# One-core Fourier mixing plus feed-forward kernel: pair 0 takes both slots through step B before mixing, and step B's loads change queue

## The chip, the cores and the metric

The kernel runs on one core of one Trainium2 chip. The metric is device time in microseconds of one execution, lower being better: the median of three runs, 1337.13 us before the change (1335.86 to 1338.55). The profile comes from one more execution of the same program.

## The reference, cut to what matters

```python
def _attn_ref(x, w_r, w_i, b_r, b_i):           # x: (4, 3008, 256)
    X = np.fft.rfft(x, axis=1)
    Yr = Xr @ w_r - Xi @ w_i + b_r
    Yi = Xr @ w_i + Xi @ w_r + b_i
    Yr, Yi = sign(Y) * max(abs(Y) - 0.01, 0)      # each of the two
    return np.fft.irfft(Yr + 1j * Yi, n=3008, axis=1)

def _moe_ref(x, w_in, w_out, alpha):             # x: (12032, 256)
    h = x @ w_in                                  # 2048 wide
    g = max(h, 0) + alpha * min(h, 0)
    return g @ w_out
```

A Fourier transform along the sequence, a complex 256 by 256 mix of the channels, a shrink by 0.01 towards zero, the transform back, and a two-layer feed-forward block. `w_in` and `w_out` arrive as 64-bit floats, and the kernel turns them into two 32-bit parts on the chip.

## The kernel before, in words

The sequence of 3008 is 47 x 64, so the transform is made in two steps. Step A (`a_load`, `a_mm`, `a_evac`, lines 339 to 406) multiplies groups of x rows by the 47-point table; for batch 0 its result stays on chip in `a0_s`, for the other batches it goes to DRAM (`ad`). Step B (`b_load`, `b_mm`, `b_evac`, `b_evac2`, lines 410 to 506) brings rows of it, 128 partitions at a time, into a tile `bt` (three buffers) and multiplies by a 64-point table `rb_s`. The 24 frequencies ("slots") are taken two at a time, as 12 pairs q. `m_mm` (line 508) mixes the channels of a pair, `m_evac` (line 542) shrinks, `c_mm` (line 588) takes the pair back through the 64-point table `cf_s`, and `c_evac` (line 606) copies it out and stores it to DRAM (`zd`). Step D then reads `zd` back for the feed-forward block, which fills the rest of the time.

The order of work is written out by hand, engine by engine, and every engine and every DMA queue runs what it was given in that order. Around the change it is this:

- Step A of batch 0 runs over 16 groups (loop at line 997). In the middle of it, `b_half(0, 0)` and `b_half(1, 0)` load the first halves of the row tiles of pairs 0 and 1 by GpSimd (POOL); after it, the second halves go by SyncE (SP), followed on SP by x rows of batch 1, table rows 4 to 11 of `rb_s`, and one `conv_load`. `b_load(0, 2)` goes by POOL.
- `keep_warm(WARM)` gives TensorE (PE) 38 small matmuls, and then the loop at line 1031 runs t = 0 to 12. At t = 0, `first_pair` (line 439) does pair 0: slot 0 (four matmuls, then two ScalarE and two VectorE instructions that split the result into a high and a low part), ten small matmuls, the bias, the mix of slot 0, slot 1, then step B of pair 1, and last the mix of slot 1.
- At each later t: `b_mm` of pair t, the load of pair t + 3, `c_evac` of pair t - 4 with its store, `b_evac` of pair t, `m_evac` of pair t - 2, `m_mm` of pair t - 1, `b_evac2` of pair t, `c_mm` of pair t - 3, and `pump(PT[t])`. At t = 1 four matmuls of step A of batch 1 are put in.
- `pump(n)` (line 310) emits n of the instruction groups that convert the weights. One piece of weights (a 512 KB load by `conv_load` on SP, into one of three buffers) takes four groups, and two pieces overlap: group 1 is VectorE L288 of the older piece with ScalarE L270 of the newer, group 2 is VectorE L271 of the newer, group 3 is ScalarE L282 and L283, VectorE L284 and GpSimd L285 of the older, group 4 is L291 (VectorE or GpSimd) and GpSimd L292 of the older with VectorE L272 of the newer. The very first piece has only its three first groups. `PT` says how many groups each t gets: 0, 0, then 3 for t = 2 to 10, and 4 at t = 11.
- `load_cf` (line 210) brings table parts for `c_mm` at t = 0, 3, 6 and 8, by POOL. `load_rb` brings table parts for step B at t = 3 and 5, by SP.
- After the loop `TAIL` runs the last evacuations and `c_mm` of pairs 10 and 11, and ten groups of step A of batch 1 (`a_fill`). Then the feed-forward steps begin, and what is left of the conversion is pumped into their first 32 (`PAT`, line 965); at step 23 `combine_mix` (line 224) makes the weights of the mix for the later batches.

Of the kernel before, what the change touches and what calls it, by code (L numbers as in the profile page):

```python
# [96 lines left out]
def fft_mix_moe(ctx, tc, x, w_r, w_i, b_r, b_i, w_in, w_out, alpha, la, rb, lc, rd, lf, cf, sel, out):  # L97
    nc = tc.nc
# [27 lines left out]
    def f(t):  # L126
        return t.bitcast(F32)
# [16 lines left out]
    cf_s = f(cw_s)  # L144
# [63 lines left out]
        nc.sync.dma_start(out=rb_s[:, n0:n1], in_=rb[:, n0 + at:n1 + at])  # L208

    def load_cf(n0, n1):  # L210
        nc.gpsimd.dma_start(out=cf_s[:, n0:n1], in_=cf[:, n0:n1])

    def load_lc():
        lc_s = const.tile([128, 2, NSLOT, 128], F32R, tag="lc", name="lc_s")
# [32 lines left out]
    def conv_load():  # L247

        m, i = divmod(conv_m[0], 2)
        conv_m[0] += 1  # L250
        k = conv_m[0] % 3
        raw = cw_s[:, NSLOT + 8 * k:NSLOT + 8 * k + 8].rearrange("p (k n) f -> p k (n f)", k=2)
        raw = raw.rearrange("p k (n w) -> p k n w", w=2)
        src = w_out.bitcast(U32)[256 * m:256 * m + 256] if i else w_in.bitcast(U32)[:, 512 * m:512 * m + 512]
        nc.sync.dma_start(out=raw.rearrange("p k n w -> p k (n w)"), in_=src.rearrange("(k p) f -> p k f", p=128))
        conv_raw.append((raw, m, i))
# [151 lines left out]
    bt, xs, xe, yc, ys = {}, {}, {}, {}, {}  # L408

    def b_half(q, h):  # L410
        if h == 0:
            bt[0, q] = work.tile([128, 2, C], F32, tag="bt", name="bt", bufs=3)
        src = a0_s.rearrange("(w s q) (h g) r c -> q h w s (g r) c", w=4, s=2, h=2)[q, h]
        for k in range(2):
            (nc.sync if h else nc.gpsimd).dma_start(out=bt[0, q][64 * h:64 * h + 64, k], in_=src[:, k])

    def b_load(b, q):
        t = work.tile([128, 2, C], F32, tag="bt", name="bt", bufs=3)
        if b == 0:
            src = a0_s.rearrange("(w s q) g r c -> q w s (g r) c", w=4, s=2)[q]  # L420
        else:
            src = ad[b].rearrange("(w s q) r c -> q w s r c", w=4, s=2)[q]

        for k in range(2):
            (nc.gpsimd if b == 0 else nc.sync).dma_start(out=t[:, k], in_=src[:, k])
        bt[b, q] = t

    def b_slot(t, ps, q, s):
        for ct in range(CT):
            PE.matmul(ps[:, s, ct], t[:, s, 128 * ct:128 * ct + 128], rb_s[:, 2 * q + s], start=True, stop=True)  # L430

    def b_mm(b, q):
        t = bt.pop((b, q))
        ps = ps_f.tile([128, 2, CT, 128], F32, tag="f", name="ps_b")
        for s in range(2):
            b_slot(t, ps, q, s)
        pb[b, q] = ps

    def first_pair():

        t = bt.pop((0, 0))
        ps = ps_f.tile([128, 2, CT, 128], F32, tag="f", name="ps_b")
        pm[0, 0] = pm0 = ps_h.tile([128, 2, C], F32, tag="h", name="ps_m")
        hi, lo = (work.tile([128, 2 * CT * 192], F32R, tag=tag, name=tag).rearrange("p (s k n) -> p s k n", s=2, k=CT)
                  for tag in ("Xh", "Xl"))

        def slot(s):
            b_slot(t, ps, 0, s)
            up, down = (slice(64, 192), slice(0, 64))
            A.activation(out=hi[:, s, :, up], in_=ps[:, s], func=AF.Copy)  # L450
            A.activation(out=hi[:, s, :, down], in_=ps[:, s, :, 64:128], func=AF.Copy, scale=-1.0)
            V.tensor_tensor(out=lo[:, s, :, up], in0=ps[:, s], in1=f(hi)[:, s, :, up], op=ALU.subtract)
            V.scalar_tensor_tensor(out=lo[:, s, :, down], in0=ps[:, s, :, 64:128], scalar=-1.0,
                                   in1=f(hi)[:, s, :, down], op0=ALU.mult, op1=ALU.subtract)

        def mixed(s):
            n = 0
            for a, ws in ((hi, 2), (lo, 1)):
                for i, o in ((0, 64), (1, 0)):
                    for ct in range(CT):  # L460
                        for w in range(ws):
                            n += 1
                            PE.matmul(pm0[:, s], a[:, s, ct, o:o + 128], mix[i][:, w, ct],
                                      start=False, stop=(s == 1 and n == 6 * CT))

        slot(0)
        keep_warm(MID)
        PE.matmul(pm0, *bias[0], start=True, stop=False)
        mixed(0)
        slot(1)  # L470
        b_mm(0, 1)
        b_evac(0, 1)
        mixed(1)

    def b_evac(b, q):
        ps = raw = pb.pop((b, q))
        hi = work.tile([128, 2 * CT * 192], F32R, tag="Xh", name="Xh")
        lo = work.tile([128, 2 * CT * 192], F32R, tag="Xl", name="Xl")
        xs[b, q] = hi, lo, ps
        if b == 0:  # L480
            hi, lo = (t.rearrange("p (s k n) -> p s k n", s=2, k=CT)[:, :, :, 64:192] for t in (hi, lo))
        else:
            hi, lo = (t[:, 0:512].rearrange("p (k s n) -> p s k n", s=2, n=64) for t in (hi, lo))
            ps = ps.rearrange("p s k (w n) -> p s (k w) n", w=2)
        A.activation(out=hi, in_=ps, func=AF.Copy)
        sv = None
        if b:
            sm = work.tile([128, 256], F32, tag="ot", name="sm", bufs=1)
            sv = sm, sm.rearrange("p (k s n) -> p s k n", s=2, k=CT)
            A.activation(out=sv[1], in_=raw[:, :, :, 64:128], func=AF.Copy)  # L490
        xe[b, q] = hi, lo, ps, sv
# [114 lines left out]
    def c_evac(b, q):  # L606
        ps = pc.pop((b, q))
        st = work.tile([128, 2, C], F32, tag="zst", name="zst", bufs=3)
        aside = b == 0 and q == NPAIR - 2
        if aside:  # L610
            V.tensor_copy(out=st, in_=ps)
        else:
            A.activation(out=st, in_=ps, func=AF.Copy)
        zdone.append(q)
        dst = zd[b][8 * q:8 * q + 8].rearrange("(s q) r c -> (q r) s c", s=2)
        if b == 0:
            (nc.sync if aside else nc.scalar).dma_start(out=dst, in_=st)
        else:
            stores.append((dst, st))

# [345 lines left out]
    NG = R // 2  # L966
    EARLY = 4
    FILL = 14
    C0 = 1
    PT = [0, 0, 3, 3, 3, 3, 3, 3, 3, 3, 3, 4]  # L970
    TAIL = [['me', 1], ['ce', 3], ['cm', 2], ['cm', 1], ['ce', 2], ['ce', 1], ['d'], ['f', 4], ['e'], ['f', 6]]
    WARM = 38
    MID = 10
    A1_TAGS = ("zst", "zst", "Yt", "zst", "bt", "bt", "bt", "Xh", "Xl", "Xh", "Xl", "zst", "zst", "Yc")
    X1_TAGS = {4: ("Yl", "Yl"), 5: ("os", "Yt"), 6: ("gl",) * 2}
    idle = const.tile([128, 128], BF16, name="idle")
# [1 line left out]
    def keep_warm(n):  # L978
        ps = ps_f.tile([128, 512], F32, tag="f", name="ps_idle")
        for _ in range(n):  # L980
            PE.matmul(ps[:, 0:128], idle, idle, start=True, stop=True)

    with tc.manual_schedule():
# [13 lines left out]
        for n, (b, g) in enumerate(seq):  # L997
            a_mm(b, g)
            if n >= 1:
                a_evac(*seq[n - 1])  # L1000
            if n == NG // 2:
                b_half(0, 0)
                b_half(1, 0)
            if n == NG:
                b_half(0, 1)
                b_half(1, 1)
                b_load(0, 2)
                a_load(1, 1)
                load_rb(4, 12)
                for _ in range(C0):  # L1010
                    conv_load()
                bias_parts()
        a_evac(*seq[-1])
        split_mix()
# [3 lines left out]
        def run(fn, q, *args):  # L1018
            if 0 <= q < NPAIR:
                fn(0, q, *args)  # L1020
# [10 lines left out]
        for t in range(NPAIR + 1):  # L1031
            if t == 0:
                first_pair()
            elif t > 1:
                run(b_mm, t)
            run(b_load, t + 3)
            run(c_evac, t - 4)
            if t > 1:
                run(b_evac, t)
            run(m_evac, t - 2)  # L1040
            if t > 1:
                run(m_mm, t - 1, ps_h)
            for g in range(2, EARLY) if t == 1 else ():
                a_mm(1, g)
                a_evac(1, g)
            if t:
                run(b_evac2, t)
            run(c_mm, t - 3)
            if t < NPAIR:
                pump(PT[min(t, len(PT) - 1)])  # L1050
            if t in (3, 5):
                load_rb(3 * t + 3, 3 * t + 9)
            if t in (0, 3, 6, 8):
                load_cf((t + 1) // 3 * 6, (t + 1) // 3 * 6 + 6)
            if t == 3:
                put()
            if t == 6:
                load_tables()
            if 7 <= t < 12:
                a_load(1, t - 5)  # L1060
            if t == NPAIR - 1:
                load_rb(0, 4)
            if t == 10:
                half(1)
                conv_m[1] = FT
# [159 lines left out]
        for k in range(len(spairs) + SLAG):  # L1225
# [7 lines left out]
            if k >= SLAG:  # L1233
                n, t = spairs[k - SLAG]
# [43 lines left out]
```

## Time and profile before

| what | value |
|---|---|
| median of three runs | 1337.13 us |
| the three runs | 1338.55, 1335.86, 1337.13 us |
| the profiled execution's own time | 1335.1 us |
| its span, first to last instruction | 1333.3 us |
| mean granted TensorE clock | 1.00 of full |

The span is 1.8 us shorter than the profiled execution's time, and that execution is 2.0 us below the median. Times in the rows are microseconds from the start of the span. In a timeline the first number is the start, the second the duration (first start to last end for several instructions), then the engine, the line of the kernel, the operation, the tiles written and read, the shapes and the count; a bracket gives idle time of the engine just before and what ended it. PE is TensorE's matmuls, PEld its weight loads, DVE VectorE, ACT ScalarE, POOL GpSimd, SP SyncE.

### The profile page before, as it was taken

The numbers are of one execution on the slowest core, as the hardware profiler recorded it, in microseconds if no ns is written. First come the engines' busy times: TensorE is split into PE (matmuls) and PEld (weight loads), VectorE is DVE, ScalarE is ACT, GpSimd is POOL, SyncE is SP. The second block draws the span as 40 slices with busy tenths as digits, with TensorE's granted clock in tenths as the row PEclk, the third lists the DMA queues.
The fourth block names the chain that finished last, engine by engine and source line by source line (L and its number), as shares of the span: only waits on it lengthen the run. The fifth ranks groups of instructions, "written<-read, shape, count | busy, mean of one in ns | idle before, by whom it ended". The sixth has DMA issues, their size and how long they took to land.

```text
span 1333.3 us, 22169 instructions
## 1 busy us (share of the span) xinstructions
PE 1322.0 (99%) x7868; PEld 1155.6 (87%) x7868; DVE 1045.5 (78%) x1858; ACT 729.8 (55%) x1442; POOL 381.4 (29%) x364
## 2 busy tenths in 40 slices
PE   9999999999999999999999999999999999999998
PEld 5977888888888888888789888988898889888988
DVE  3767866777787877687777888888888888888885
ACT  3566654655456554444555555555555555555654
POOL 3754652212221222221222222222222222222222
PEclk9999999999999999999999999999999999999999
DMA  8974333332243312121101101110111011101000
GB/s 220 255 219 136 108 107 103 118 117 78 72 134 96 111 65 72 52 76 36 37 13 40 28 10 32 29 29 10 31 29 29 10 31 29 29 10 31 17 16 25
DMA packets 103759, 89.74 MB, mean 67 GB/s; under 512 B 62446, under 2 KB 85849, under 8 KB 103648
## 3 DMA queue, kind: packets, MB, share of 16 engines
q1 hardware_dynamic: 95744, 77.68, 20.4%
q0 software_dynamic: 4912, 7.76, 2.1%
q10 hardware_dynamic: 2992, 2.88, 0.7%
q8 instruction: 62, 1.02, 0.3%
q14 instruction: 49, 0.40, 0.1%
HBM read 50.76 MB, written 34.34 MB: 64 GB/s over the span
## 4 chain that ended last, share of the span: by engine, by line
PE 90%; DVE 5%; issue 2%; ACT 1%; DMA 1%; SPq 0%; ACTq 0%; DVEq 0%
PE ps_h L712 37%; PE ps_o L739 10%; PE ps_o L737 10%; PE ps_o L738 10%; PE ps_m L534 6%; PE ps_d L633 4%; PE ps_o L906 3%; PE ps_b L430 2%; PE ps_a L387 2%; DVE q L724 1%; DMA rb_s<-tab_rb 1%; PE ps_c L602 1%; PE ps_c L603 1%; DVE conv L272 1%; PE ps_c L604 1%
## 5 line engine op out<-in xcount | busy, mean ns | idle before, releaser
L712 PE MATMUL ps_h<-yh,w 128*128 128x512 f32 (+1 forms) x1472 | 492.4, 389 | 2.4 <-DVE sq L811 1.6
L712 PEld LDWEIGHTS ps_h<-yh,w 128*128 128x128 f32 x1472 | 275.1, 188 | 58.2 <-DVE q L724 3.2
L712 PE MATMUL ps_h<-yl,w 128*128 128x512 f32 (+1 forms) x736 | 284.9, 387 | 0.0
L840 POOL TENSOR_TENSOR l<-t,h 128x512 fp32r<-128x512 f32 x98 | 127.0, 1296 | 449.7 <-ACT h L838 430.2
L811 DVE SCALAR_TENSOR_TENSOR sq<-sq,beta_s,ps_h 128x512 f32<-128x512 f32 (+1 forms) x240 | 166.2, 724 | 59.1 <-ACT sq L810 58.8
L726 ACT ACTIVATE gh<-q 128x512 fp32r<-128x512 f32 x144 | 91.0, 632 | 160.7 <-DVE q L724 160.7
L729 POOL TENSOR_TENSOR gl<-q,gh 128x512 fp32r<-128x512 f32 x69 | 93.4, 1354 | 255.8 <-ACT gh L726 193.7
L712 PEld LDWEIGHTS ps_h<-yl,w 128*128 128x128 f32 x736 | 138.9, 189 | 21.7 <-DVE yl L684 0.2
L724 DVE SCALAR_TENSOR_TENSOR q<-q,beta_s,ps_h 128x512 f32<-128x512 f32 x144 | 107.0, 743 | 61.2 <-ACT q L723 59.8
L810 ACT ACTIVATE sq<-ps_h 128x512 f32<-128x512 f32 (+1 forms) x240 | 131.8, 577 | 31.0 <-PE ps_h L712 27.1
L826 ACT ACTIVATE dh<-sq 128x768 fp32r<-128x768 f32 x98 | 83.0, 847 | 108.5 <-DVE sq L811 81.3
L723 ACT ACTIVATE q<-ps_h 128x512 f32<-128x512 f32 x144 | 85.3, 592 | 79.9 <-PE ps_h L712 77.8
L838 ACT ACTIVATE h<-t 128x512 fp32r<-128x512 f32 x98 | 62.0, 633 | 105.2 <-DVE t L836 101.8
L737 PE MATMUL ps_o<-gh,w 128*128 128x512 f32 x288 | 114.5, 398 | 0.0
L739 PE MATMUL ps_o<-gl,w 128*128 128x512 f32 x288 | 112.7, 391 | 0.3 <-POOL gl L729 0.3
L738 PE MATMUL ps_o<-gh,w 128*128 128x512 f32 x288 | 112.8, 392 | 0.0
L835 DVE TENSOR_TENSOR dl<-sq,dh 128x768 fp32r<-128x768 f32 x98 | 93.2, 951 | 0.0
L729 DVE TENSOR_TENSOR gl<-q,gh 128x512 fp32r<-128x512 f32 x75 | 60.0, 800 | 42.3 <-ACT gh L726 41.5
L739 PE MATMUL ps_o<-l,sw_a 128*128 128x256 f32 x294 | 82.7, 281 | 0.0
L737 PE MATMUL ps_o<-h,sw_a 128*128 128x256 f32 x294 | 82.0, 279 | 0.0
L832 DVE TENSOR_TENSOR t<-sq 128x512 f32<-128x512 f32 x98 | 67.6, 690 | 2.9
L839 DVE TENSOR_TENSOR l<-t,h 128x512 fp32r<-128x512 f32 x98 | 67.0, 684 | 0.0
(199 smaller groups left out, 2969.7 us busy)
## 6 DMA issues: line engine op xcount, KB each, us to landing
zt<-zd SPq DMA_DIRECT2D x32, 384.0 KB
zd<-zst SPq DMA_DIRECT2D x37, 256.0 KB
ad<-ast SPq DMA_DIRECT2D x48, 192.0 KB
bt<-ad SPq DMA_DIRECT2D x72, 128.0 KB
out<-oT SPq DMA_DIRECT2D x248, 32.0 KB
xt<-in_x SPq DMA_DIRECT2D x21, 320.0 KB
cw_s<-in_moe_w_in SPq DMA_DIRECT2D x8, 512.0 KB
cw_s<-in_moe_w_out SPq DMA_DIRECT2D x8, 512.0 KB
```

The lines of the kernel that those rows point to most:

```text
L712: PE.matmul(ps, wi_h[m // FH][:, w, ct, 128 * (m % FH):128 * (m % FH) + 128], a[ct][:, 0:n], start=(k == 0), stop=(k == 3 * CT - 1))
L723: A.activation(out=q, in_=ps, func=AF.Relu, scale=-1.0)
L724: V.scalar_tensor_tensor(out=q, in0=q, scalar=beta_s[:, m:m + 1], in1=ps, op0=ALU.mult, op1=ALU.add)
L726: A.activation(out=hi, in_=q, func=AF.Copy)
L729: return lambda: (V if by_v else G).tensor_tensor(out=lo, in0=q, in1=f(hi), op=ALU.subtract)
L737: PE.matmul(o, wh, gh, start=first, stop=False)
L738: PE.matmul(o, wl, gh, start=False, stop=False)
L739: PE.matmul(o, wh, gl, start=False, stop=last)
L810: A.activation(out=q[:, j], in_=ps, func=AF.Relu, scale=-1.0)
L811: V.scalar_tensor_tensor(out=q[:, j], in0=q[:, j], scalar=beta_s[:, m:m + 1], in1=ps, op0=ALU.mult, op1=ALU.add)
L835: V.tensor_tensor(out=dl, in0=q[:, HS:], in1=f(dh), op=ALU.subtract)
L840: G.tensor_tensor(out=l24, in0=t24, in1=f(h24), op=ALU.subtract)
```

## The change

Seven edits.

1. `b_half`: pair 0's second half goes by POOL, and only pair 1's stays on SP.
2. `b_load`: from pair 3 on the rows of batch 0 go by SP instead of POOL. `load_cf`: the three later table parts go by SP instead of POOL.
3. `first_pair`: slot 0, six small matmuls instead of ten, slot 1, bias, mix of slot 0, mix of slot 1, and then step B of pair 1.
4. `c_evac`: the stores of pairs 6 and 7 (at t = 10 and 11) are issued by POOL instead of ACT.
5. The first `conv_load` moves from ahead of the loop to t = 0, behind the row load of pair 3.
6. `PT` gives t = 1 three groups instead of none, so that each later t has the groups that t + 1 had, and t = 11 has groups 4, 1, 2, 3 where it had 1, 2, 3, 4. The conversion after the loop has four groups less to do.
7. `C0` and its loop go.

```diff
     def load_cf(n0, n1):
-        nc.gpsimd.dma_start(out=cf_s[:, n0:n1], in_=cf[:, n0:n1])
+        (nc.sync if n0 else nc.gpsimd).dma_start(out=cf_s[:, n0:n1], in_=cf[:, n0:n1])
...
         for k in range(2):
-            (nc.sync if h else nc.gpsimd).dma_start(out=bt[0, q][64 * h:64 * h + 64, k], in_=src[:, k])
+            (nc.sync if h and q else nc.gpsimd).dma_start(out=bt[0, q][64 * h:64 * h + 64, k], in_=src[:, k])
...
         for k in range(2):
-            (nc.gpsimd if b == 0 else nc.sync).dma_start(out=t[:, k], in_=src[:, k])
+            (nc.gpsimd if b == 0 and q < 3 else nc.sync).dma_start(out=t[:, k], in_=src[:, k])
...
         slot(0)
         keep_warm(MID)
+        slot(1)
         PE.matmul(pm0, *bias[0], start=True, stop=False)
         mixed(0)
-        slot(1)
+        mixed(1)
         b_mm(0, 1)
         b_evac(0, 1)
-        mixed(1)
...
-            (nc.sync if aside else nc.scalar).dma_start(out=dst, in_=st)
+            (nc.sync if aside else nc.gpsimd if 6 <= q < 8 else nc.scalar).dma_start(out=dst, in_=st)
...
-    C0 = 1
-    PT = [0, 0, 3, 3, 3, 3, 3, 3, 3, 3, 3, 4]
+    PT = [0, 3, 3, 3, 3, 3, 3, 3, 3, 3, 3, 4]
...
-    MID = 10
+    MID = 6
...
                 load_rb(4, 12)
-                for _ in range(C0):
-                    conv_load()
                 bias_parts()
...
             run(b_load, t + 3)
+            if t == 0:
+                conv_load()
             run(c_evac, t - 4)
```

## Rows read from the trace of the kernel before

**Rows 1.** The page's first part: busy time of each engine.
```profile
PE 1322.0 (99%) x7868; PEld 1155.6 (87%) x7868; DVE 1045.5 (78%) x1858; ACT 729.8 (55%) x1442; POOL 381.4 (29%) x364
```

**Rows 2.** The timeline of PE from pair 0's first slot on.
```profile
23.27 0.67 PE L430 MATMUL ps_b<-rb_s,bt 128*128 128x128 f32 x4
23.78 0.72 PE L981 MATMUL ps_idle<-idle 128*128 128x128 bf16 x10
24.31 0.48 PE L468 MATMUL ps_m<-bias_p,ones 128*128 128x512 f32 x1
24.62 0.64 PE L463 MATMUL ps_m<-wr_s,Xh 128*128 128x256 f32 x4
...
28.80 0.72 PE L463 MATMUL ps_m<-wr_s,Xh 128*128 128x256 f32 x4
...
30.30 1.88 PE L387 MATMUL ps_a<-xt,lf_s 94*96 94x512 f32 x4
32.02 1.06 PE L430 MATMUL ps_b<-rb_s,bt 128*128 128x128 f32 x8
32.83 0.48 PE L514 MATMUL ps_m<-bias_p,ones 128*128 128x512 f32 x1
...
38.08 0.71 PE L430 MATMUL ps_b<-rb_s,bt 128*128 128x128 f32 x4 [0.84 <-DMA bt<-a]
...
41.70 1.03 PE L596 MATMUL ps_c<-Y,cw_s 128*128 128x256 f32 x4
42.56 1.05 PE L430 MATMUL ps_b<-rb_s,bt 128*128 128x128 f32 x8
...
47.39 1.05 PE L430 MATMUL ps_b<-rb_s,bt 128*128 128x128 f32 x8
...
61.89 1.05 PE L430 MATMUL ps_b<-rb_s,bt 128*128 128x128 f32 x8
...
67.23 1.05 PE L430 MATMUL ps_b<-rb_s,bt 128*128 128x128 f32 x8
```

**Rows 3.** Waits from 20 to 40 us: total us, times, longest.
```profile
PE ps_b L430 <- DMA bt<-a: 1.9, 4, 0.8
```

**Rows 4.** DMA issues by POOL near 1.3, 14 and 21 us: us to landing.
```profile
lf_s<-tab_lf POOLq DMA_DIRECT2D x1, 35.2 KB, 2.9
...
bt<-a POOLq DMA_DIRECT2D x4, 64.0 KB, 7.3
...
bt<-a POOLq DMA_DIRECT2D x2, 128.0 KB, 4.6
```

**Rows 5.** The timeline of POOL where pair 2's rows are issued.
```profile
20.87 1.34 POOL L425 DMA_DIRECT2D bt<-a  x2 [4.32 <-issue]
```

**Rows 6.** Waits from 60 to 66 us.
```profile
PEld ps_m L521 <- POOL Xh L500: 0.3, 1, 0.3
```

**Rows 7.** Timelines of DVE and of ACT, t = 8 and t = 11.
```profile
66.80 0.68 DVE L291 TENSOR_TENSOR conv<-conv,w 128x512 f32<-128x512 f32 x1
...
68.06 2.35 DVE L288 SCALAR_TENSOR_TENSOR conv<-cw_s,conv 128x512 uint32<-128x512 uint32 x1
...
81.64 0.81 DVE L288 SCALAR_TENSOR_TENSOR conv<-cw_s,conv 128x512 uint32<-128x512 uint32 x1
...
85.68 0.68 DVE L548 SCALAR_TENSOR_TENSOR Y<-ps_m,Yc 128x512 f32<-128x512 f32 x1
...
82.48 0.63 ACT L282 ACTIVATE w<-conv 128x512 fp32r<-128x512 f32 x1 [2.01 <-DVE conv L288]
...
84.61 0.69 ACT L547 ACTIVATE Yc<-ps_m,lam_s 128x512 f32<-128x512 f32 x1 [0.44 <-ACT zst L613]
```

**Rows 8.** Waits from 160 to 184 us.
```profile
PEld ps_h L712 <- DVE q L724: 2.0, 4, 0.6
```

**Rows 9.** Stretch of only SP row loads (batch 1): engines' us, clock, DMA, GB/s.
```profile
164.00:167.00 3.00, 3.00 (x14) 2.17 (x13) 2.97 (x6) 1.19 (x3) 0.97 (x2) 1.00 0.24 81
```

**Rows 10.** The same view over four pairs of the loop, t = 4 to 7.
```profile
42.00:61.00 19.00, 19.00 (x148) 18.43 (x147) 16.13 (x22) 12.32 (x21) 16.13 (x20) 1.00 0.92 234
```

## The prediction

> **What bounds the kernel now.** I read the page's first part, then the timeline of PE from pair 0 on, then the waits of that stretch. PE is busy 99% of the span [rows 1], so time can only come out of holes in PE's own sequence or out of work taken from it. From t = 4 on PE runs pair after pair without a hole: the first matmuls of pairs 4 and 5 stand 4.83 us apart, from 42.56 to 47.39 [rows 2], and that is what the matmuls need. Before that PE is late. The path from slot 0 to pair 4, piece by piece [rows 2]: a slot 0.51 (23.27 to 23.78), ten small matmuls 0.53, the bias 0.31, one mix 1.50 (28.80 to 30.30), step B of a pair 0.81 (32.02 to 32.83), four matmuls of step A 1.72 (30.30 to 32.02). One pair of the loop is 4.83, or 3.97 without its `c_mm` (0.86, from 41.70 to 42.56). In the old order that is 2 x 0.51 + 0.53 + 0.31 + 2 x 1.50 + 0.81 + 1.72 + 3.97 + 4.83 = 16.19, but the rows stand 19.29 apart. So 3.1 us are waits, and the largest cause named is rows of `bt` that have not landed [rows 3], last at 38.08 for pair 3 [rows 2]. Later holes, at t = 8, t = 12 and about 175 us, are read with the parts that touch them.
>
> **The change, part by part.** The terms are called A to E.
>
> **A, the start (edits 1, 2, 3, 5).** The new order is the old path with six small matmuls for ten, 0.32 for 0.53, and is 15.98 long. Slot 1 now runs while ScalarE and VectorE split slot 0, and pair 1's rows are asked for after both mixes, so those loads get 3 us more. Pair 3's rows are issued by SP behind slot 1, ahead of the weights instead of behind three loads of them. If nothing waits, 3.1 + 0.2 = 3.3 us go. What is late next is slot 0 itself: its second half now goes by POOL. POOL's next issue stood at 20.87 [rows 5]; the halves move to this place. From issue to landing POOL's loads took 2.9 us for 35 KB, 4.6 for 128 KB, and 7.3 for 64 KB while x was still being loaded [rows 4]. Between the first two by size, 64 KB land 3.4 later, at 24.3, against the old start of 23.27: 1.0 us lost. I take this because x is in by then. Slot 1's half is issued 0.67 later (half of 1.34 [rows 5]) and is asked for 0.83 later, so it is covered. A = -3.3 + 1.0 = -2.3; with 2.9 it is -2.8, with 4.6 it is -1.1, with 7.3 it is +1.6.
>
> [...]
>
> Pair 2's rows by POOL start 1.34 us later, at 22.2, and land near 26.8 by the 4.6 [rows 4, 5]; they are asked for at 24.3 + 0.51 + 0.32 + 0.51 + 0.31 + 3.00 + 0.81 + 1.72 = 31.5. Pair 3's are issued near 25.6 and asked for at 35.5. Both are covered.
>
> **B, POOL relieved (edit 2).** From pair 8 to pair 9 the cycle is longer: 61.89 to 67.23 is 5.34, 0.5 over 4.83 [rows 2], and the wait named is for POOL's negation of the high part [rows 6], which in the code stands behind a table load (t = 6) and a row load (t = 7) on POOL. Both leave POOL. B = -0.5; at least 0.
>
> **C, the last pairs (edits 4, 6).** At t = 11 the groups come as 4, 1, 2, 3. ScalarE's L282 waits for VectorE's L288, and behind it on ScalarE stand the copy of pair 8 and the shrink of pair 10, on which the last two `c_mm` wait with nothing else for PE to do. In the old order L288 came first, 81.64 to 82.45, L282 began at 82.48 and the shrink (L547) at 84.61, while VectorE came to its part (L548) at 85.68 [rows 7]. Where group 4 comes first, at t = 8, L288 ended 3.61 after L291 began (66.80 to 70.41), 2.80 later than with L288 first. L547 then ends at 84.61 + 2.80 + 0.69 = 88.1, 2.4 after 85.68. Against it: L288 itself was held to 2.35 there, 1.5 above the 0.81 of t = 11 [rows 7], with a GpSimd instruction beside it that ran late behind POOL's loads; and the store of pair 7 leaves ScalarE, about 0.4. POOL has no such loads now, so I take 1.0 of the 1.5 and all of the 0.4 off: 2.4 - 1.0 - 0.4 = +1.0. Ends: 0 and +2.4. POOL pays for two stores (0.67 each by [rows 5]) where it no longer has row loads: nothing.
>
> **D, four groups less after the loop (edit 6).** From 160 to 184 us the weight loads of L712 wait 2.0 us in four places for VectorE [rows 8]; that is where the last pieces of weights and `combine_mix` want VectorE, ScalarE and GpSimd together. With the conversion over some three steps sooner they no longer meet. Weight loads run ahead of the matmuls, so 2.0 is an upper end; D = -1.0, ends -2.0 and 0. The three groups at t = 1 cost PE nothing as long as their weights are there: ScalarE and VectorE have no more than one pair's split to do.
>
> **E, what SP now carries (edits 2, 5).** SP's queue gets nine pairs' rows (256 KB each) and three table parts, between the weights, x rows and stores of `ast` that it had. Each row load waits for a free `bt`, and the weights stand behind it; if they are late, ScalarE stands at L270 with the split of the next pair behind it. What a row load costs by SP shows in batch 1, where for 3 us nothing else moved: 0.24 of the 16 engines busy and 81 GB/s [rows 9], so as if four engines worked, and 256 KB take about 3.2 us. Over t = 4 to 7 the engines were 0.92 busy at 234 GB/s [rows 10], of which POOL's rows were 256 KB in 4.83 us, 54 GB/s. The rest is 0.92 x 180 / 234 = 0.71; if it is even over the engines, those four get 0.71 + 3.2 / 4.83 = 1.37 of a pair, 1.8 us too much in each of six pairs (t = 3 to 8), 10.7 in all. Against it, busy time includes waiting for one another, rows are asked for three pairs (14.5 us) after their issue, and weights about 1.3 pairs (6.4 us) after theirs. Of the two ends, 0 and 10.7 less the 3.4 that are left of those 6.4 after a landing of 3, 7.3, I take the lower with a little of the upper: E = +0.7.
>
> [...]
>
> **Sum.** -2.3 - 0.5 + 1.0 - 1.0 + 0.7 = -2.1. The profiled execution took 1335.1 us (1333.3 of span), so it would take 1333.0. It stands 2.0 below the median of 1337.1, and the forecast for the median is 1335.0. The runs of before lie 2.7 us apart, 0.2%, which is also about what a measurement of this kernel tells from no change.
>
> **Rivals.**
> - **Faster: C and E cost nothing.** Without POOL's loads VectorE is not held and reaches the last groups early, and the row loads hide in their three pairs of lead. For: PE has no hole from 42 to 61 us although the engines were 0.92 busy [rows 10]. Against: the order of the groups at t = 11 is fixed, and L282 is behind L288 in any case. The sum is -2.3 - 0.5 - 1.0 = -3.8: 1333.3.
> - **Slower: the row loads fill their four engines.** Place: t = 7 to 11. Price: E at 7.3 instead of 0.7, 1341.6. It decides once those engines have over 4.83 + 3.4 / 6 = 5.4 us of work per pair; by [rows 9, 10] it is 1.37 x 4.83 = 6.6 if all busy time is work, and (0.66 + 0.47) x 4.83 = 5.5 if a third of the 0.71 is waiting, so the point is near. Against: the lead of three pairs, and that PE had no hole while all 16 engines stood at 0.92.
> - **Slot 0 late.** The first halves, on the same queue, took 7.3 us [rows 4]. If the second do, A is +1.6 and the time 1338.9. Against: x had been loaded by 20 us.
>
> **How the numbers follow.** Forecast 0.45, the faster rival 0.38, the slower 0.10, slot 0 late 0.07. Faster by over 0.2% is 0.38; within it are the forecast and most of the last, 0.50; slower 0.12. The range takes A at -2.8, D at -2.0 and C and E at 0, 1331.8, and on the other side slot 0 late, 1338.9. Outside are the slower rival and as much again.
>
> **What would show it.** A: pair 4's first matmul near 40.3 instead of 42.56, slot 0 near 24.3, no wait for `bt` at pair 3. B: cycles of 4.83 throughout. C: the last `c_mm` about 1 us further behind pair 11's mix than before. D: no wait of L712 between 165 and 180. E: no ScalarE wait at L270 for weights. Wrong would be slot 0 after 25.5, cycles of over 5 us at t = 7 to 11, or a wait of PE for `bt` after pair 3.

## The result, and the profile after

| | before | after |
|---|---|---|
| median, us | 1336.86 (6 runs, 1335.17 to 1338.55) | 1350.57 (6 runs, 1347.46 to 1357.7) |
| ratio | | 1.0107, 95% interval 1.0081 to 1.0134 |
| span of the profiled execution, us | 1333.3 | 1345.7 |

The change costs 13.7 us, 1.1%. The forecast was 1335.0, and its range ended at 1338.9. The profiled execution of after is the quickest of its six (1347.46 us), so what follows explains 12.4 us of span.

The busy time of PE is 2.6 us above that of [rows 1]: the work is the same, and the time went into holes (stretches in which PE waits) and, for a small part, into matmuls at a lower clock (0.64 from 28 to 32 us, 0.50 from 56 to 60).

The first part of the page of after:
```profile
PE 1324.6 (98%) x7864; PEld 1159.8 (86%) x7864; DVE 1044.1 (78%) x1857; ACT 731.2 (54%) x1442; POOL 371.7 (28%) x348
```

To see where, set the same work of both kernels side by side. The timeline of PE of after, as in [rows 2]:
```profile
24.52 0.68 PE L430 MATMUL ps_b<-rb_s,bt 128*128 128x128 f32 x4 [0.87 <-issue]
...
26.78 0.68 PE L430 MATMUL ps_b<-rb_s,bt 128*128 128x128 f32 x4 [1.24 <-DMA bt<-a]
27.22 0.58 PE L469 MATMUL ps_m<-bias_p,ones 128*128 128x512 f32 x1
...
31.90 1.05 PE L430 MATMUL ps_b<-rb_s,bt 128*128 128x128 f32 x8
...
43.29 1.05 PE L430 MATMUL ps_b<-rb_s,bt 128*128 128x128 f32 x8
...
62.63 1.05 PE L430 MATMUL ps_b<-rb_s,bt 128*128 128x128 f32 x8
...
72.29 1.05 PE L430 MATMUL ps_b<-rb_s,bt 128*128 128x128 f32 x8
77.12 1.05 PE L430 MATMUL ps_b<-rb_s,bt 128*128 128x128 f32 x8
...
88.28 1.05 PE L430 MATMUL ps_b<-rb_s,bt 128*128 128x128 f32 x8
...
112.08 3.76 PE L633 MATMUL ps_d<-rd_s,zt 96*128 96x94 f32 x32
```
Three rows of the same view of the kernel before that did not stand in [rows 2] (pairs 6 and 11, and step D):
```profile
52.22 1.05 PE L430 MATMUL ps_b<-rb_s,bt 128*128 128x128 f32 x8
...
76.89 1.05 PE L430 MATMUL ps_b<-rb_s,bt 128*128 128x128 f32 x8
...
98.14 3.76 PE L633 MATMUL ps_d<-rd_s,zt 96*128 96x94 f32 x32
```

| first matmul of | before | after | later by | since the row above |
|---|---|---|---|---|
| slot 0 | 23.27 | 24.52 | 1.25 | |
| pair 4 | 42.56 | 43.29 | 0.73 | -0.52 |
| pair 6 | 52.22 | 62.63 | 10.41 | **+9.68** |
| pair 9 | 67.23 | 77.12 | 9.89 | -0.52 |
| pair 11 | 76.89 | 88.28 | 11.39 | +1.50 |
| step D | 98.14 | 112.08 | 13.94 | **+2.55** |
| end of span | 1333.3 | 1345.7 | 12.4 | -1.5 |

Nearly eight tenths of the net loss stand between pairs 4 and 6. The waits of after from 48 to 58 us name the chain:
```profile
ACT zst L613 <- DMA ad<-ast: 7.0, 1, 7.0
DVE Y L548 <- ACT Yc L547: 6.9, 1, 6.9
PEld ps_m L514 <- DVE Y L548: 6.2, 1, 6.2
PE ps_m L514 <- DVE Y L548: 6.0, 1, 6.0
```
Read it from the bottom: PE's mix waits for VectorE's shrink, that for ScalarE's, and ScalarE stands at L613, the copy of pair 0 out of PSUM. L613 needs one of the three `zst` buffers. Groups 0, 1 and 3 of step A of batch 1 sit in them (`A1_TAGS`) until their stores `ad<-ast` have landed. These stores are `put()` at t = 3, on SP. The timeline of SP of after shows what they stood behind:
```profile
39.55 1.15 SPq L425 DMA_DIRECT2D bt<-a  x2
42.98 0.37 SPq L255 DMA_DIRECT2D cw_s<-in_moe_w_out  x1
43.40 0.46 SPq L208 DMA_DIRECT2D rb_s<-tab_rb  x1
43.91 0.43 SPq L211 DMA_DIRECT2D cw_s<-tab_cf  x1
44.38 3.64 SPq L334 DMA_DIRECT2D ad<-ast  x4
```
Before, the same four stores were issued at 28.61 and L613 ran at 43.11 without a wait. Now they come 15.8 us later, behind row loads that wait for a free `bt` and behind a piece of weights whose buffer ACT L283 gave back only at 42.3 to 43.0 (ScalarE had stood 3.37 us before it for another piece). Once issued they were slow too: from the first issue to L613 (53.12) it is 8.74 us. Three stretches of 1 us inside the hole (busy time by engine, then granted clock, DMA share, GB/s):
```profile
51.00:52.00 1.00, 0.00 (x0) 0.00 (x0) 0.00 (x0) 0.00 (x0) 0.00 (x0) 1.00 0.28 110
52.00:53.00 1.00, 0.00 (x0) 0.00 (x0) 0.00 (x0) 0.00 (x0) 0.00 (x0) 1.00 0.26 101
53.00:54.00 1.00, 0.00 (x0) 0.00 (x0) 0.00 (x0) 0.60 (x1) 0.00 (x0) 1.00 0.26 97
```
Every compute engine waits, and the DMA engines are a quarter busy. That looks like SP's row loads in [rows 9] (0.24 at 81 GB/s), but from 51 to 53 us no row load moves. A row load puts 1 KB into each partition, and when row loads moved alone, from 41 to 43 us, all 181 packets were under 2 KB; these stores move 2 KB per partition, the table parts ahead of them 3 KB. From 51 to 53 us the only packets under 2 KB are 19 that are also under 512 B, too small for a row load's 1 KB. The packets of 51 to 53 us, and below them those of 41 to 43 us, when row loads moved alone:
```profile
DMA packets 107, 0.21 MB, mean 106 GB/s; under 512 B 19, under 2 KB 19, under 8 KB 107
...
DMA packets 181, 0.18 MB, mean 91 GB/s; under 512 B 4, under 2 KB 181, under 8 KB 181
```
What stood behind row loads in SP's queue was itself down to a quarter of the engines (0.26 to 0.28). Whether these are the engines that the row loads had kept busy stays open: the trace does not name engines.

After the hole the granted clock, 1.00 from 51 to 54 us, was at 0.50:
```profile
56.00:60.00 4.00, 3.80 (x17) 3.71 (x18) 3.86 (x6) 2.76 (x5) 3.10 (x3) 0.50 0.66 202
```

The other places: the waits of ACT of after from 24 to 104 us show ScalarE standing for weights seven times; between pairs 9 and 11 that is 1.50 us of PE's time.
```profile
ACT conv L270 <- DMA cw_s<-in_moe_w_in: 10.0, 4, 4.1
ACT zst L613 <- DMA ad<-ast: 7.0, 1, 7.0
...
ACT conv L270 <- DMA cw_s<-in_moe_w_out: 5.7, 3, 3.4
```
And from 160 to 184 us, where [rows 8] had 2.0 us:
```profile
PEld ps_h L712 <- DVE q L724: 0.2, 1, 0.2
```

### The profile page after: what moved, and what is told of

Same layout as the page of the kernel before. It is cut to its first block, busy times and chain, and to the rows that moved or that the text cites. A ratio compares the mean times of both kernels' runs of the same rounds, so it can differ in the third digit from the quotient of the medians.

```text
span 1345.7 us, 22143 instructions
## 1 busy us (share of the span) xinstructions
PE 1324.6 (98%) x7864; PEld 1159.8 (86%) x7864; DVE 1044.1 (78%) x1857; ACT 731.2 (54%) x1442; POOL 371.7 (28%) x348
## 4 chain that ended last, share of the span: by engine, by line
PE 93%; DVE 3%; DMA 2%; ACT 1%; issue 1%; SPq 0%; ACTq 0%; POOL 0%; DVEq 0%
PE ps_h L712 37%; PE ps_o L739 11%; PE ps_o L737 11%; PE ps_o L738 11%; PE ps_m L534 6%; PE ps_d L633 4%; PE ps_b L430 3%; PE ps_o L906 3%; PE ps_a L387 2%; PE ps_m L521 1%; DMA ad<-ast 1%; PE ps_c L602 1%; PE ps_c L603 1%; PE ps_c L604 1%; DVE q L724 1%
## 5 line engine op out<-in xcount | busy, mean ns | idle before, releaser
L712 PE MATMUL ps_h<-yh,w 128*128 128x512 f32 (+1 forms) x1472 | 492.2, 389 | 2.1 <-DVE sq L811 1.6
L712 PEld LDWEIGHTS ps_h<-yh,w 128*128 128x128 f32 x1472 | 275.1, 188 | 57.4 <-DVE q L724 2.3
L712 PE MATMUL ps_h<-yl,w 128*128 128x512 f32 (+1 forms) x736 | 284.9, 387 | 0.0
L712 PEld LDWEIGHTS ps_h<-yl,w 128*128 128x128 f32 x736 | 138.9, 189 | 21.7 <-DVE yl L684 0.2
```

The source lines that it names most:

```text
L712: PE.matmul(ps, wi_h[m // FH][:, w, ct, 128 * (m % FH):128 * (m % FH) + 128], a[ct][:, 0:n], start=(k == 0), stop=(k == 3 * CT - 1))
```

## The experiments

Each kernel was timed in five rounds beside the kernel before; medians are in us, and each ratio is to the kernel before.

**1. The stores earlier, by POOL.** The first theory: the stores' place on SP is the cause.
```
 after:  -            if t == 3:
         -                put()
         +            if t == 1:
         +                put(nc.gpsimd)
```


> The changed kernel with the four stores of step A (ad<-ast) issued at t = 1 by POOL instead of at t = 3 by SP. Theory 1, the stores stand on SP behind row loads and weights and hold the zst buffers: the hole of PE from 50 to 56 us goes whole, the wait of ACT L613 for ad<-ast goes, pair 6 starts near 53 us instead of 62.88, and the time falls by 7.6 to 9.7 us, to 1341 to 1343. Theory 2, SP's row loads fill their engines and make the weights late, and the stores are only the wait that happened to end last: ACT stands at L270 for weights instead, a hole of 3 us or more stays between pairs 4 and 6, and the time stays above 1346.

Measured: 1348.25, ratio 1.0102 (1.0071 to 1.0133). The hole went: pair 6 starts at 55.01. But by step B of pair 11 (87.47) the gain is down to 0.8 us of after's 88.28. (The profiled execution, 1356.16, is 8 us above the median; it lost them at a lower clock, 0.62 from 98 to 104 us and 0.50 from 104 to 116, see the last section.) The waits of ACT from 24 to 104 us:
```profile
ACT conv L270 <- DMA cw_s<-in_moe_w_in: 12.0, 4, 4.4
ACT conv L270 <- DMA cw_s<-in_moe_w_out: 11.4, 4, 4.5
```
15.7 us of waiting for weights became 23.4. Theory 1 was right about the hole and wrong about the time: two lines of supply were late, and the stores had hidden the weights.

**2. Edit 1 undone.**
```
 after:  -(nc.sync if h and q else nc.gpsimd)
         +(nc.sync if h else nc.gpsimd)
```


> The changed kernel with the second half of pair 0's rows by SP again (edit 1 undone). Theory 1, the start lost 1.25 us on slot 0, 1.24 on the wait for slot 1 and 1.3 on mixes at the lower clock, and the hole at 50 to 56 us follows from the chain that begins with step B of pair 1, so it moves with the start: slot 0 at 23.3, granted clock 1.00 from 27 to 32, pair 4 near 39.5, pair 6 near 59, time 1347 (3.8 lower). Rival, the hole's end is set by SP's transfers and not by PE: pair 4 near 39.5 but pair 6 still at 62 to 63, time within 1 us of 1350.6.

Measured: 1351.47, ratio 1.0113 (1.01 to 1.0126). Slot 0 came at 23.97, but slot 1 waited 3.40 for its rows instead of 1.24, the clock was 0.60 from 28 to 32, and pair 4 came at 44.92. The time is the rival's, but neither theory's reasons held; slot 1's rows come later by SP than by POOL here. What did follow the start is the hole: pair 6 at 64.80, as far behind pair 4 (19.9) as in after (19.3).

**3. Edit 2 undone.**
```
 after:  b_load   -(nc.gpsimd if b == 0 and q < 3 else nc.sync)
                  +(nc.gpsimd if b == 0 else nc.sync)
         load_cf  -(nc.sync if n0 else nc.gpsimd)
                  +nc.gpsimd
```


> The changed kernel with row loads and table parts of batch 0 by POOL again (edit 2 undone); the other six edits stay. Theory 1: SP reaches the stores of ast before 40 us, the hole at 50 to 56 goes (8.7), the waits for weights at L270 shorten (some 2.5 at t = 10 and 11), and the 0.5 at t = 8 comes back: 1339.9. Rival, the new order of pair 0 and the later weights are at fault: the hole or one like it stays and the time is above 1346.

Measured: 1341.06, ratio 1.0037 (1.0025 to 1.0049). With the other six edits in place, edit 2 is 9.5 of the 13.7 us. ACT's waits at L270 fell to 0.4. But a hole of 2.7 us stayed at the same place, and the timeline of SP says why:
```profile
39.10 0.37 SPq L255 DMA_DIRECT2D cw_s<-in_moe_w_out  x1
39.52 0.47 SPq L208 DMA_DIRECT2D rb_s<-tab_rb  x1
40.03 4.78 SPq L334 DMA_DIRECT2D ad<-ast  x4
```
With edit 6 the conversion runs a step ahead, so at t = 3 it already asks for the fourth piece of weights, which must wait for ACT L283 (38.42). Before, that piece was asked for after the stores (43.25 against 28.61).

**4. Edit 3 alone.**
```
 before: first_pair in the new order, MID = 6
```


> The kernel before with edit 3 alone (both slots, then the mixes, six small matmuls). Term A of the prediction: pair 4 starts up to 3.3 us before 42.56; as pair 3's rows are still asked for by POOL behind the table part, about half of it, so 41.0 and 1335.4. Rival, the order itself leaves PE idle at the start, the granted clock falls in the mixes as in the changed kernel, and pair 4 is not before 42.5: 1336.9 or more.

Measured: 1336.18, ratio 1.0 (0.9991 to 1.0008). Level with the kernel before, as the rival had it, but not for its reason: the clock stayed at 1.00, but slot 1, now asked for right after slot 0, stood 2.60 us for its rows. From slot 0 to pair 4 it is 19.35 us (24.13 to 43.48), against 19.29 before.

**5. Edit 2 undone, and the stores at t = 1 on SP.**
```
 run 3:  put() at t == 1 instead of t == 3
```


> The changed kernel with rows and table parts by POOL (edit 2 undone, 1341.1) and the four stores of ast by SP at t = 1 instead of t = 3. Theory 1, what still holds the zst buffers there is edit 6: the piece of weights that it asks for a step sooner waits on SP for ACT L283, and the stores stand behind it at 40.03: the hole of 2.85 us goes with the 1.7 us of lower clock after it, and the time falls by 3.5 to 4.5 us to 1336.6 to 1337.6, with a tail 2 us longer and 160 to 184 us 1.6 shorter than before. Rival, the wait returns elsewhere as it did with the first move of the stores: above 1339.

Measured: 1338.36, ratio 1.0023 (1.001 to 1.0035): 2.7 less, where 3.5 to 4.5 were expected. The hole is gone, and pair 6 stands at 51.28, 9.67 behind pair 4, two pairs of 4.83. But the stores now stand ahead of the third piece of weights, for which ACT waits 4.0 us, and the two pairs from 6 to 8 take 11.55 us (51.28 to 62.83). Most of what is left of the loss is in the tail: step B of pair 11 is 0.43 us behind the kernel before (77.32), step D 4.19 (102.33). ACT's timeline at t = 11:
```profile
85.69 0.68 ACT L282 ACTIVATE w<-conv 128x512 fp32r<-128x512 f32 x1 [3.27 <-DVE conv L288]
```

**6. Row loads cut by source partition.**
```
 run 1, b_load from pair 3 on:
   for w in range(4):
       nc.sync.dma_start(out=t[32 * w:32 * w + 32, k], in_=src[w:w + 1, k])
```


> The kernel with the stores by POOL at t = 1, and each row load by SP from pair 3 on cut into eight of one source partition each instead of two of four. Theory A, two row loads run on four engines only, and weights wait behind them on these four while twelve stand idle: stretches of a us at a DMA share of 0.25 to 0.29 vanish between 40 and 80 us, ACT waits at L270 fall from 23.4 us to under 8, and the time falls by 3 us or more below 1348. Theory B, the weights are late because SP reaches them late, behind row loads that wait for a free bt and take SP's time to issue: with four times the instructions the waits at L270 are as long or longer and the time is 1348 or more.

Measured: 1360.07, ratio 1.0182 (1.0168 to 1.0195). ACT waits 34.5 us at L270. That is theory B's result, but the kernel does not decide: SP needed 5 to 8.4 us to issue a pair's eight loads, more than a pair lasts, so a new limit covered the question. It shows one thing more. Two stretches of 1 us:
```profile
54.00:55.00 1.00, 1.00 (x7) 1.00 (x6) 0.60 (x2) 0.47 (x2) 0.00 (x0) 0.50 0.70 52
...
72.00:73.00 1.00, 1.00 (x9) 0.93 (x8) 0.00 (x0) 0.82 (x2) 0.67 (x2) 1.00 0.79 52
```
The row loads of after, alone from 41 to 43 us, for comparison:
```profile
41.00:43.00 2.00, 2.00 (x17) 1.95 (x16) 0.76 (x2) 1.81 (x4) 0.00 (x0) 1.00 0.27 91
```
Three times as many engines count as busy, and they move little more than half as much. The 52 GB/s is what SP issued: eight loads of 32 KB in 5.07 us (from 29.66).

**7. The row loads by ACT.** The same loads, the same source, another queue.
```
 run 1, b_load from pair 3 on:  nc.sync -> nc.scalar
```


> The kernel with the stores by POOL at t = 1, and the row loads from pair 3 on issued by ACT instead of SP (same two loads per pair, same source); the weights stay on SP. Theory A, weights stand in one line with row loads on SP's queue: with the rows on another queue ACT waits for weights at L270 fall from 23.4 us to under 5, and the time comes to 1338 to 1340, near the 1338.4 with rows by POOL. Theory B, the four engines that a row load runs on have too little capacity for rows, weights and stores together, whatever queue asks: the waits at L270 stay over 12 us and the time at 1344 or more.

Measured: 1350.23, ratio 1.0125 (1.0098 to 1.0152). ACT's waits for weights at L270 fell from 23.4 us to 1.0 (first row), although a stretch in which the DMA engines are a quarter busy is still there (second row):
```profile
ACT conv L270 <- DMA cw_s<-in_moe_w_in: 1.0, 1, 1.0
...
44.00:48.00 4.00, 2.90 (x13) 2.80 (x14) 2.76 (x5) 2.56 (x5) 1.44 (x3) 0.67 0.27 92
```
Pairs 4 to 11 took 39.0 us (50.66 to 89.61) against 44.6 in run 1 (42.90 to 87.47), so the weights were on time at a higher pace. In run 1 they are late, then, because they stand in one line with row loads; at run 7's pace the engines have the capacity, and whether they would have it at the 34.3 us that the kernel before takes for these pairs no run shows. Nor does the run part the two ways of standing in line: in SP's order of issue, behind a load that waits for a free `bt` (the first three pieces were issued at 28.95, 32.87 and 35.71 in run 1, at 25.81, 26.64 and 27.23 here), and on the engines, behind the bytes of a row load. The 23.4 and 1.0 us fit both, and no run tests either alone. The time did not follow, since ACT now stood while it issued:
```profile
34.58 4.53 ACTq L425 DMA_DIRECT2D bt<-a  x4
39.22 0.59 ACT L404 ACTIVATE ast<-ps_a 96x512 f32<-96x512 f32 x1 [4.25 <-DMA ad<-ast]
```
The bracket names a store, but the 4.25 us are those of the four loads above it. PE's next mix waited 3.62 us behind them (pair 3 at 39.85, pair 4 at 50.66).

**8. PE kept busy before slot 1.**
```
 after:  -    MID = 6
         +    MID = 24
```


> The changed kernel with 24 small matmuls instead of 6 between slot 0 and slot 1, where PE waits 1.24 us for rows. If the lower clock in the two mixes of pair 0 (0.64 from 28 to 32 us) comes from PE standing idle there, it is 1.00 with PE kept busy, pair 4 starts 1.3 us sooner after slot 0 (17.5 us instead of 18.8), and the time falls by about 1.3 to 1349.3. If not, the clock in 28 to 32 stays near 0.64.

Measured: 1349.43, ratio 1.0112 (1.0087 to 1.0137). The clock is 1.00 where after had 0.64 (first two rows run 8, last row after):
```profile
24.00:28.00 4.00, 3.81 (x42) 3.65 (x43) 1.12 (x4) 1.11 (x4) 0.07 (x1) 1.00 1.04 196
28.00:32.00 4.00, 4.00 (x29) 3.17 (x27) 0.62 (x2) 0.86 (x2) 0.40 (x1) 1.00 0.95 284
...
28.00:32.00 4.00, 4.00 (x25) 4.00 (x24) 0.62 (x2) 0.05 (x1) 0.00 (x0) 0.64 0.96 285
```
and pair 3 starts 12.17 us after slot 0 instead of 13.95. Of these 1.8 us 1.7 were lost again one pair later, where the mix waits for VectorE while ScalarE stands 2.8 us for weights: pair 4 is 18.69 us behind slot 0, not 17.5 (18.77 in after). The median moved by 1.1, less than the runs are apart, so that it meets the 1349.3 of the expectation is luck.

**9 to 11. The gains alone.**
```
 w1 = before:  PT = [0, 4, 3, ...]; put() at t == 2 instead of 3
 w2 = w1:      load_cf by SP from its second part on
 w3 = w1:      load_cf by SP at t = 6 only; conv_m = [0, CL + 1]
```


> The kernel before with four groups of the weight conversion at t = 1 (so the groups keep their places at t = 8 and 11) and the stores of ast by SP at t = 2 instead of 3. Term D alone: the waits at L712 from 160 to 184 us go (1.6 us), nothing is lost at t = 5 as the stores stay ahead of the blocked piece of weights, and the tail stays as before: 1334.6. If the order of the groups in the last steps is not what lengthened the tail of the changed kernel, the tail is 2 us longer here too and the time 1336.6.

> The same with the three later table parts by SP (half of edit 2). Term B: the 0.5 us at t = 8 goes as POOL has one load less there: 1334.1. If the table parts on SP hold the weights up, ACT waits at L270 and the time is 1335 or more.

> The kernel before with four groups of conversion at t = 1, the stores of ast at t = 2, only the table part of t = 6 by SP, and the ninth piece of weights allowed one step sooner. The waits at L712 from 160 to 184 us go (1.6), the cycle at t = 8 is 4.83 to 5.1 (0.3 to 0.5), and the late piece of weights in the tail of the last version (1.2) does not come: 1334.3. If the places it is won in are given back elsewhere, as they were with the two versions before it, it is 1335.3 or more.

Measured: w1 1336.02, ratio 0.9999 (0.999 to 1.0008); w2 1335.3, 0.9992 (0.9983 to 1.0001); w3 1336.15, 0.9999 (0.9991 to 1.0008). In all three the waits of L712 from 160 to 184 us are 0.2, as in after, and none is measurably faster. In w1 most of the gain is given back at t = 8, where PE waits 1.3 us for POOL's negation: pairs 8 to 9 take 6.53 us (62.75 to 69.28) instead of 5.34. In w2 that is 5.59, and ACT waits 7.0 for weights at L270; in w3 it is 5.95, where 4.83 to 5.1 were expected.

**12. The groups at their old places.**
```
 run 5:  PT = [0, 4, 3, ...] instead of [0, 3, 3, ...]
```


> The changed kernel with rows and table parts by POOL, the stores of ast by SP at t = 1, and four groups of conversion at t = 1 instead of three, so that at t = 11 VectorE's L288 comes first again, as before the change. Theory (term C): the tail's wait of 2.4 us, where L282 on ACT stands behind a late L288, shrinks to 0.5, and the time falls by about 2 from 1338.4 to 1336.0 to 1336.6, level with the kernel before. Rival, what is left of the loss is in edits 1, 3, 4 or 5: the tail shortens or not, and the time stays at 1338 or more.

Measured: 1335.16, ratio 0.9996 (0.9987 to 1.0005): 3.2 less than run 5. At t = 11 L282 waits half as long, PE's waits for `Y` in the tail fall from 2.3 us to 0.3, and the loss is used up. Part of it lay behind the wait of 2.3: the last L613 of the tail stood 2.40 us for PE's `c_mm` in run 5 (until 92.94), and 1.46 here (until 89.75).
```profile
83.45 0.67 ACT L282 ACTIVATE w<-conv 128x512 fp32r<-128x512 f32 x1 [1.63 <-DVE conv L288]
```

The chain 1350.57, 1341.06, 1338.36, 1335.16 takes off edit 2, then the place of the stores, then the phase of the groups. The other edits stay in run 12, and it is level with the kernel before. No version tried is measurably faster than that kernel: the two lowest medians, run 12 and w2, have intervals that hold 1.0.

## Why the prediction was wrong

**E failed, and with it the forecast.** E was +0.7, with ends at 0 and 7.3. What happened stood there: row loads at a quarter of the engines (0.27 in after), weights behind them, ScalarE at L270 (15.7 us). Three things went wrong in it.
- The price took only the weights as being behind the row loads. The step lists "stores of `ast` that it had" among SP's load and then does not ask who waits for them. They hold `zst` buffers that `c_evac` needs at t = 4. Between pairs 4 and 6 that was 9.68 us of PE's time, and no end of the range held it. Run 1 gives only 2.3 us of the median back, because the weights were late too, and each of the two waits covered the other.
- The value was put near the lower end because of the leads, and the slower rival was held at 10% because PE had no hole while all engines stood at 0.92 [rows 10]. That row was of POOL's row loads, on another queue than the weights. Run 7 against run 1 shows that rows on another queue than the weights' leave the weights on time (ACT waits 1.0 us at L270 instead of 23.4).
- Leads of 14.5 us for rows and 6.4 for weights were counted from the issue order of before. With row loads in SP's line a piece of weights is issued only when a `bt` is free: the piece of 34.17 let ACT L270 start only at 41.19.

The slower rival ("the row loads fill their four engines") had one of the right waits, ACT at L270, at 10%. Its place (t = 7 to 11) was too late and its price 6.6 us above the forecast instead of 15.6.

**Edit 6 cost time in a place that no term had.** The step on D says: "The three groups at t = 1 cost PE nothing as long as their weights are there". It did not ask what the piece of weights that is now asked for sooner stands ahead of. Run 3 shows it: the four stores, which cost a hole of 2.69 us with no row load on SP; run 5, with the stores moved, is 2.7 us lower.

**A: -2.3 forecast, +0.73 in the trace.** Slot 0 came at 24.52, forecast 24.3: right. The other profiled executions point the same way, though the ranges overlap: 24.19 to 25.93, mean 25.0, in eight kernels with that half by POOL, and 23.27 to 25.25, mean 24.2, in six with it by SP. The 23.27 of [rows 2] was the earliest of the six. What failed is slot 1 ("so it is covered"): it waited 1.24. The argument compared issue times and assumed equal landing. Second, the two mixes with their bias took 4.68 us (27.22 to 31.90) instead of 3.31, at a granted clock of 0.64. Run 8, with PE busy for 3.81 us of 24 to 28 instead of 2.24, had 1.00, but so had runs 1 and 3 with 2.03 and 1.90: that the idle time before them lowers the clock is not shown. 1.24 + 1.37 are 2.6 of the 2.8 us by which the path (18.77) is longer than the 15.98 of the forecast. In run 12 it is 17.01. That `bt` is not waited for at pair 3 was right.

**B: -0.5, right.** Pairs 8 to 9 take 4.83 in after (72.29 to 77.12). With POOL's loads back and four groups at t = 1 it was 6.53 in w1 and in run 12 (61.82 to 68.35). In after PE was some 10 us late there, so how much of it POOL's relief gives by itself no run shows.

**C: +1.0 forecast, about +2.5.** The order of the groups at t = 11 was read rightly, and the upper end, 2.4, was the value: run 5 has PE waits of 2.3 us with POOL's loads back in their old place, and run 12, where L288 comes first again, takes 2.0 of them away. The 1.0 that was taken off, on the estimate that a GpSimd instruction late behind POOL's loads had held L288 up, was only in part there: without those loads L288 took 1.66 us in after (94.97 to 96.63, with POOL's L292 beside it again, 94.62 to 96.07), 0.7 under the 2.35 of [rows 7] and 0.85 over the 0.81. What makes it long no run shows. In after the weights were late besides: L270 stood 3.68 us for them and ran from 96.14, as L288 came to its end (94.97 to 96.63), so that either would have held L282 up.

**D: -1.0 forecast, -1.5 in the trace, right.** The wait of L712 is 0.2, and so it is in runs 3, 5 and 12 and in w1 to w3. The gain did not show in a time of its own: in w1 to w3 it was given back.

**Sum.** By the trace +0.73 + 9.68 - 0.52 + 1.50 + 2.55 - 1.54 = 12.4, against -2.1.

## What to carry to other kernels

When a load moves to another queue, write down that queue in order, with the buffer each entry waits for and the buffer each entry frees, stores included: a store that comes late holds its buffer, and the wait shows on an engine that has nothing to do with the change (here ACT, 7.0 us at L613). A wait that is removed can uncover a second one of the same size (run 1: ACT's waits at L270 went from 15.7 us to 23.4), so undo the whole edit before pricing its parts. A step of software pipelining more also moves which request stands first at a later point (runs 3 and 12).

## What the runs showed of the hardware

- **Weights behind row loads on one queue came late.** With rows and weights on SP's queue ACT waited 23.4 us for weights, with the same rows on ACT's queue 1.0 (runs 1 and 7). How much of it is SP's order of issue and how much the order on the engines stays open.
- **A busy share is not a rate.** Row loads from four source partitions kept 0.27 of the engines busy at 91 GB/s; cut to one partition each, 0.70 to 0.79 at 52, about what SP issued (run 6).
- **Issuing took time.** Four row loads held ACT for 4.53 us (run 7; a single one at 46.36 us took 0.54), and eight of 32 KB took SP 5 to 8.4, waits included (run 6).
- **The clock after a hole was not the same in two executions.** In after PE waited 2.33 us before a `c_mm` at 100.36, and the clock stayed at 1.00 (first row). In run 1's profiled execution PE waited 2.06 at the same place, and the clock fell to 0.62 and then stayed at 0.50 with PE fully busy again (the other rows); from 122 to 126 us it was back at 1.00.
```profile
104.00:110.00 6.00, 6.00 (x15) 2.28 (x14) 0.78 (x2) 4.94 (x10) 1.65 (x2) 1.00 0.65 186
...
98.00:104.00 6.00, 5.22 (x11) 2.98 (x12) 3.14 (x6) 1.99 (x4) 2.15 (x2) 0.62 0.36 126
104.00:110.00 6.00, 6.00 (x8) 1.98 (x7) 0.00 (x0) 2.60 (x6) 0.00 (x0) 0.50 0.74 185
110.00:116.00 6.00, 6.00 (x8) 1.98 (x7) 0.78 (x2) 2.66 (x6) 2.55 (x2) 0.50 0.20 58
```
  Run 1, with holes, also had the wider spread: it took from 1345.35 us (mean clock 0.999) to 1360.85 (0.987), and the kernel before, at 0.997 to 1.00, stays within some 3 us. Why the clock fell in one execution and not in the other stays open.
